# Block-diagonal products of a transformer block's training step regrouped from five 128-column blocks to six groups of whole heads

## The chip, the cores and the metric

The kernel runs on one core of one Trainium2 chip. The metric is the time of one launch on the device in microseconds (us), as the median of several executions; every execution quoted here ran at the full granted TensorE clock (1.00 in the records). Engines are named as in the profile: PE is TensorE's matmuls, PEld its weight loads, DVE VectorE, ACT ScalarE, POOL GpSimd, SP SyncE; a q behind a name is that engine's DMA queue.

## The reference, cut to what matters

One sequence of S = 2048 rows and D = 640 columns goes through a linear-attention block (32 heads of 20 columns) and a gated feed-forward block. The outputs are the result and the gradients of all inputs.

```python
def _A_ref(x, wqkv, wo):                       # H = 32, Dh = 20
    q, k, v = ...                              # x @ wqkv, cut into heads
    pq, pk = phi(q), phi(k)
    kv  = jnp.einsum("bhsd,bhse->bhde", pk, v) # one 20 x 20 block for each head
    z   = jnp.einsum("bhsd->bhd", pk)
    num = jnp.einsum("bhqd,bhde->bhqe", pq, kv)
    den = jnp.einsum("bhqd,bhd->bhq", pq, z)[..., None] + 1e-6
    return (num / den) ... @ wo
...
h  = x + _A_ref(_layernorm(x), A_wqkv, A_wo)
h2 = h + _B_ref(_layernorm(h), B_w_gate, B_w_up, B_w_down)
# outputs: h2 and its vjp for x, wqkv, wo, w_gate, w_up, w_down
```

The kernel never makes v. It uses that kv is a 640 x 640 matrix with 32 small blocks on its diagonal, KV, and folds it into weights: W2 = KV wo (forward), WK2 = dKV wv-transposed (backward), and the weight gradients dwo = KV-transposed G and dwv = Y dKV, where Y and G are sums over the sequence.

## The kernel before: the parts concerned

The 640 columns are cut into five blocks of 128. A head has 20 columns, so 128-column blocks cut heads: every block has to be multiplied with all blocks that share a head with it, and each of these matmuls streams full chunks of 320 columns, mostly against zeros.

```python
def head_range(i):                      # heads that block i touches
    h_lo = (i * P) // Dh
    h_hi = (i * P + P - 1) // Dh
    return Dh * h_lo, min(D, Dh * (h_hi + 1))
def overlapping(c0, c1):
    return [i for i in range(DT) if not (head_range(i)[1] <= c0 or head_range(i)[0] >= c1)]
...
for i in range(DT):                     # W2: 26 matmuls of 320 columns
    js = overlapping(i * P, (i + 1) * P)
    ps = mm("ps_w2")
    mm_row(ps, lambda k: KVT[:, js[k], i * P:(i + 1) * P], lambda k, n0, n1: wo[:, js[k], n0:n1], len(js))
    nc.scalar.copy(out=half(W2[:, i, :]), in_=row(ps))
dm(3)                                   # three tiles of dm = dh2 wd^T, ready work for PE
...
for t in range(ST + 2):                 # the loop behind it, on 16 tiles
    if t < ST:
        ...
        mm_row(ps, ..., lambda i, n0, n1: W2[:, i, n0:n1], DT)      # ps_a
        nc.vector.tensor_tensor(out=half(xr[:]), in0=row(ps), in1=half(xr[:]), op=ALU.add)
        nc.scalar.dma_start(out=scr_h1_v[:, t, :], in_=xr[:])       # store of the first residual
        ...
        dm(1)                           # ten matmuls and a ScalarE eviction
...
def dwo(j):                             # 26 matmuls of 320 in all; dwv is alike, with 30
    is_ = overlapping(j * P, (j + 1) * P)
    ps = mm("ps_dwo")
    mm_row(ps, lambda k: KV[:, is_[k], j * P:(j + 1) * P], lambda k, n0, n1: G[:, is_[k], n0:n1], len(is_))
    nc.scalar.copy(out=half(ev[:]), in_=row(ps))
```

`mm` takes the next of four PSUM accumulators in turn.

Of the kernel before, what the change touches and what calls it, by code (L numbers as in the profile page):

```python
# [20 lines left out]
def kernel(  # L21
# [69 lines left out]
    scr_KVT = dram.tile([D, D], BF16, name="scr_KVT")  # L91
# [4 lines left out]

    def head_range(i):
        h_lo = (i * P) // Dh
        h_hi = (i * P + P - 1) // Dh
        return Dh * h_lo, min(D, Dh * (h_hi + 1))  # L100

    def overlapping(c0, c1):
        return [i for i in range(DT) if not (head_range(i)[1] <= c0 or head_range(i)[0] >= c1)]
# [8 lines left out]
    def mm_row(ps, lhs, rhs, n, start=True, stop=True, by_k=False):  # L112

        steps = [(ci, k) for ci in range(2) for k in range(n)]
        if by_k:
            steps.sort(key=lambda x: x[1])
        for ci, k in steps:
            nc.tensor.matmul(ps[:, ci, :320], lhsT=lhs(k), rhs=rhs(k, *NCH[ci]),  # L118
                             start=(start and k == 0), stop=(stop and k == n - 1))

# [58 lines left out]
    wvo = strips.tile([P, 2, DT, D], BF16, name="wvo", tag="S")  # L179
# [8 lines left out]
    nc.scalar.dma_start(out=x_tm[0][:, 0, 320:640], in_=x_v[:, 0, 320:640])  # L188
    w_k = A_wqkv[:, D:2 * D].rearrange("(k p) n -> p k n", p=P)
    nc.sync.dma_start(out=wqk[:, 0:3, D:2 * D], in_=w_k[:, 0:3, :])  # L190
    load_x(nc.sync, 1, 2)
# [12 lines left out]
    def load_3():  # L204
        for t0 in range(4, ST, 2):
            yield load_x(nc.sync, t0, t0 + 2)
        yield nc.sync.dma_start(out=wvo[:, 0], in_=A_wqkv[:, 2 * D:3 * D].rearrange("(k p) n -> p k n", p=P))
        yield nc.sync.dma_start(out=wvo[:, 1], in_=A_wo.rearrange("(k p) n -> p k n", p=P))
        yield load_wdT(wdT, 0)
        for c in range(4):  # L210
            yield nc.sync.dma_start_transpose(out=dh2T[:, :, c * 512:(c + 1) * 512], in_=go_flat[c * 512:(c + 1) * 512, :])
        yield load_wdT(wdT, 1)
        yield load_wdT(wdT3, 3)
# [13 lines left out]
    mask = const.tile([P, DT, 160], BF16, name="mask")  # L227
# [12 lines left out]
    wv = wvo[:, 0]  # L240
    wo = wvo[:, 1]
# [13 lines left out]
    def ln1(t):  # L255
# [6 lines left out]
        if t == 0:  # L262
            ln1_stats(1)
            wait_for(nc.scalar.copy(out=xnT[:, t, 0:3], in_=tpv[:, 0:3]), load_3())
            nc.vector.tensor_copy(out=xnT[:, t, 3:5], in_=tpv[:, 3:5])
        else:
            nc.scalar.copy(out=xnT[:, t], in_=tpv)  # L267
# [107 lines left out]
    def masks():  # L375
# [9 lines left out]
        for i in range(DT):  # L385
            e0, e1 = head_range(i)
            pm = ps[:, i // 3, (i % 3) * 160:(i % 3) * 160 + e1 - e0]
            nc.tensor.matmul(pm, lhsT=E[:H, i * P:(i + 1) * P], rhs=E[:H, e0:e1], start=True, stop=True)
        for i in range(DT):
            e0, e1 = head_range(i)  # L390
            pm = ps[:, i // 3, (i % 3) * 160:(i % 3) * 160 + e1 - e0]
            nc.scalar.copy(out=mask[:, i, :e1 - e0], in_=pm)
# [10 lines left out]
    def normalise(t):  # L403
# [8 lines left out]
        nc.vector.tensor_tensor(out=hb4(pq), in0=hb4(pq), in1=bc4(rall[:, t:t + 4, :]), op=ALU.mult)  # L412
        for tt in range(t, t + 4):
            nc.sync.dma_start_transpose(out=pqsT[:, :, tt * P:(tt + 1) * P], in_=pqa[:, tt, :])
# [8 lines left out]
    with tc.manual_schedule(engines={EngineType.PE, EngineType.DVE}):  # L423
        yk = strips.tile([P, 2, DT, D], BF16, name="yk", tag="S")
        Yt = yk[:, 0]
        KVT = yk[:, 1]
# [12 lines left out]
        nc.gpsimd.dma_start(out=mat_v(scr_Yt), in_=Yt)  # L439
        dm(1)  # L440
        for t in range(0, 12, 4):
            normalise(t)
        for t in range(3):
            load_xr(t)
        for j in range(DT):
            d0, d1 = head_range(j)
            ps = mm("ps_kvt")
            for i in range(DT):
                nc.tensor.matmul(ps[:, 0, :d1 - d0], lhsT=wv[:, i, j * P:(j + 1) * P], rhs=Yt[:, i, d0:d1],
                                 start=(i == 0), stop=(i == DT - 1))  # L450
            nc.vector.tensor_tensor(out=KVT[:, j, d0:d1], in0=ps[:, 0, :d1 - d0], in1=mask[:, j, :d1 - d0], op=ALU.mult)
        nc.gpsimd.dma_start(out=mat_v(scr_KVT), in_=KVT)
        normalise(12)

        W2 = wv
        dm(1)
        for i in range(DT):
            js = overlapping(i * P, (i + 1) * P)
            ps = mm("ps_w2")
            mm_row(ps, lambda k: KVT[:, js[k], i * P:(i + 1) * P], lambda k, n0, n1: wo[:, js[k], n0:n1], len(js))  # L460
            nc.scalar.copy(out=half(W2[:, i, :]), in_=row(ps))
        dm(3)
# [4 lines left out]
        for t in range(ST + 2):  # L467
# [16 lines left out]
            if 2 <= u <= DT + 1:  # L484
                nc.sync.dma_start(out=mat_v(scr_W2T)[:, :, (u - 2) * P:(u - 1) * P], in_=w2t)
            if 1 <= u <= DT:
                w2t = stage()[:, :DT, :]
                nc.sync.dma_start_transpose(out=w2t, in_=W2[:, u - 1, :])
# [125 lines left out]
    M = ctx.enter_context(tc.tile_pool(name="M", bufs=3))  # L614
    wpools.append(ctx.enter_context(tc.tile_pool(name="workC", bufs=7)))

    def mat(name):
        return M.tile([P, DT, D], BF16, name=name, tag="M")

# [4 lines left out]
    def tr_sb(dst, src, i):  # L624
        nc.sync.dma_start_transpose(out=dst[:, :, i * P:(i + 1) * P], in_=src[:, i, :])

    with tc.manual_schedule(engines={EngineType.SP, EngineType.Pool}):
        W2T = mat("W2T")
        nc.sync.dma_start(out=W2T[:], in_=mat_v(scr_W2T))
        woT = mat("woT")  # L630
# [69 lines left out]
    with tc.manual_schedule(engines={EngineType.SP, EngineType.DVE}):  # L700

        wqkvT = big.tile([P, 15, D], BF16, name="wqkvT", tag="B")
# [11 lines left out]
        for k in (2, 0, 1):  # L714
            for i in range(DT):
                with tc.issue_after(last_dh1T):
                    tr_piece(wqkvT[:, 5 * k:5 * k + 5, :], A_wqkv[:, k * D:(k + 1) * D], i)
# [3 lines left out]
        GT = mat("GT")  # L721
# [8 lines left out]
        dKVT = mat("dKVT")  # L730
        nc.vector.memset(dKVT[:], 0.0)
        for j in range(DT):
            d0, d1 = head_range(j)
            ps = mm("ps_dkvt")
            for i in range(DT):
                nc.tensor.matmul(ps[:, 0, :d1 - d0], lhsT=woT[:, i, j * P:(j + 1) * P], rhs=GT[:, i, d0:d1],
                                 start=(i == 0), stop=(i == DT - 1))
            nc.vector.tensor_tensor(out=dKVT[:, j, d0:d1], in0=ps[:, 0, :d1 - d0], in1=mask[:, j, :d1 - d0], op=ALU.mult)

        dzE = [wk("dzE"), wk("dzL")]  # L740
        ps = mm("ps_dz")
        for ci, (n0, n1) in enumerate(NCH):
            for t in range(ST):
                q = t % 4 * H
                nc.tensor.matmul(ps[q:q + H, ci, :320], lhsT=nS1[:, t, :], rhs=pqs_tm[:, t, n0:n1],
                                 start=(t < 4), stop=(t >= ST - 4))
        nc.vector.tensor_tensor(out=half(dzE[0][:]), in0=row(ps), in1=half(E[:]), op=ALU.mult)
# [8 lines left out]
        for i in range(DT):  # L756
            js = overlapping(i * P, (i + 1) * P)
            ps = mm("ps_wv2")
            mm_row(ps, lambda k: dKVT[:, js[k], i * P:(i + 1) * P], lambda k, n0, n1: wqkvT[:, 10 + js[k], n0:n1], len(js))
            nc.scalar.copy(out=half(WV2[:, i, :]), in_=row(ps))  # L760
            nc.sync.dma_start_transpose(out=WK2[:, :, i * P:(i + 1) * P], in_=WV2[:, i, :])
# [21 lines left out]
        G = mat("G")  # L783
# [10 lines left out]
        for t in range(ST + LAG):  # L794
# [13 lines left out]
            if 4 <= t < 4 + DT:  # L808
                tr_sb(G, GT, t - 4)
            if t == 4 + DT:  # L810
                KV = mat("KV")
            if 4 + DT <= t < 4 + 2 * DT:
                tr_piece(KV, scr_KVT, t - 4 - DT, overlapping((t - 4 - DT) * P, (t - 3 - DT) * P))
# [27 lines left out]
        dy = strips.tile([P, 2, DT, D], BF16, name="dy", tag="S")  # L841
        dKV = dy[:, 0]
        Y = dy[:, 1]

        def dwo(j):
            is_ = overlapping(j * P, (j + 1) * P)
            ev = wk("dwo", pool=j % 2)
            ps = mm("ps_dwo")
            mm_row(ps, lambda k: KV[:, is_[k], j * P:(j + 1) * P], lambda k, n0, n1: G[:, is_[k], n0:n1], len(is_))
            nc.scalar.copy(out=half(ev[:]), in_=row(ps))  # L850
            nc.gpsimd.dma_start(out=out_3[j * P:(j + 1) * P, :], in_=ev[:])

        def dwv(i):
            ev = wk("dwv", pool=1)
            ps = mm("ps_dwv")
            for ci, (n0, n1) in enumerate(NCH):
                ks = overlapping(n0, n1)
                for kk, k in enumerate(ks):
                    nc.tensor.matmul(ps[:, ci, :320], lhsT=Y[:, k, i * P:(i + 1) * P], rhs=dKV[:, k, n0:n1],
                                     start=(kk == 0), stop=(kk == len(ks) - 1))  # L860
# [11 lines left out]
        for t in range(ST):  # L872
# [22 lines left out]
            if t < DT:  # L895
                dwo(t)
            if 0 <= t - 3 < DT:
                tr_sb(dKV, dKVT, t - 3)
            if 0 <= t - 6 < DT:
                tr_piece(Y, scr_Yt, t - 6)  # L900
# [32 lines left out]
```

## Time and profile before

| | before |
|---|---|
| median, lowest, highest of 4 runs | 831.15, 831.02, 832.94 us |
| span of the profiled execution | 830.5 us |
| PE busy | 823.2 us (99%), 5533 matmuls |
| share of PE in the chain that ended last | 87% |

A kernel whose PE is busy for 99% of the span changes its time in two ways only: PE's matmuls become fewer or shorter, or PE waits less or more. So I cut the span at the starts of PE's stages. This is the windows view of the kernel before for four of them: W2 up to the first ps_a; the loop with ps_a; WK2 with the products behind it; and the last stretch with dwo and dwv. Columns: stretch, its length, busy time (and instructions) of PE, PEld, DVE, ACT, POOL, granted clock, DMA share, GB/s.

```profile
92.69:101.90 9.21, 9.21 (x58) 5.48 (x57) 6.90 (x5) 5.89 (x8) 0.00 (x0) 1.00 1.17 190
101.90:151.76 49.86, 49.86 (x322) 31.31 (x320) 33.43 (x74) 13.75 (x16) 12.91 (x30) 1.00 0.96 213
...
620.82:641.72 20.90, 20.77 (x185) 14.07 (x183) 9.25 (x25) 6.04 (x9) 1.12 (x2) 1.00 0.74 137
...
759.08:830.50 71.42, 68.66 (x520) 49.87 (x517) 13.52 (x18) 7.61 (x11) 15.04 (x28) 1.00 0.92 179
```

PE is busy for all of the first two and for all but 0.13 us of the third. (In the last, the idle 2.76 us are the tail behind the last matmul.)

### The profile page before, as it was taken

How to read it: one execution, taken by the hardware profiler on the slowest of the kernel's cores; microseconds unless marked ns; L12 is line 12 of the kernel's file. 1: busy time of each engine (PE TensorE's matmuls, PEld its weight loads, DVE VectorE, ACT ScalarE, POOL GpSimd, SP SyncE). 2: the span in 40 equal slices, each digit the busy share in tenths (PEclk: the TensorE clock that was granted, in tenths of full speed). 3: DMA queues.
4: the chain of work that ended last, by engine and by line, in shares of the span. 5: the costliest groups of instructions: out<-in, count | busy, mean ns of one | idle time of the engine just before them, and what ended most of it. 6: DMA issues, size and time to landing. Idle time of an engine off the chain costs nothing.

```text
span 830.5 us, 14069 instructions
## 1 busy us (share of the span) xinstructions
PE 823.2 (99%) x5533; PEld 527.7 (64%) x5533; DVE 446.4 (54%) x874; ACT 291.8 (35%) x414; POOL 187.4 (23%) x343
## 2 busy tenths in 40 slices
PE   8999999999999999999999999999999999999998
PEld 6766656554555555555656777777776777777776
DVE  6988766791077018800750157878874366621121
ACT  5982422670084126400831123223322133331101
POOL 2330022322312312221125302111300122113320
PEclk9999999999999999999999999999999999999999
DMA  9994889998659997994597767875597689799993
GB/s 290 210 350 105 165 181 240 281 235 202 146 118 217 211 208 154 204 242 97 109 242 172 251 171 194 213 197 165 132 230 137 110 163 169 154 245 199 216 224 89
DMA packets 281057, 158.53 MB, mean 191 GB/s; under 512 B 238976, under 2 KB 267456, under 8 KB 280992
## 3 DMA queue, kind: packets, MB, share of 16 engines
q1 hardware_dynamic: 254288, 81.30, 53.2%
q0 software_dynamic: 17888, 65.27, 25.5%
q10 hardware_dynamic: 8816, 11.08, 4.4%
q8 instruction: 43, 0.70, 0.4%
q14 instruction: 22, 0.18, 0.1%
HBM read 47.43 MB, written 53.46 MB: 121 GB/s over the span
## 4 chain that ended last, share of the span: by engine, by line
PE 87%; DVE 8%; DMA 3%; ACT 1%; issue 1%; POOL 0%; SPq 0%; ACTq 0%; DVEq 0%
PE ps_dw L590 20%; PE ps_dhn L118 14%; PE ps_dxn L824 8%; PE ps_o L886 7%; PE ps_dwqk L118 5%; PE ps_kq L118 4%; PE pg L518 4%; PE ps_dm L350 4%; PE pu L523 4%; PE ps_y L118 3%; PE ps_gt L642 3%; PE ps_dp L118 3%; PE ps_dk L118 3%; PE pdm L350 2%; PE ps_a L118 2%; DMA xr<-in_A_x_dram 1%
## 5 line engine op out<-in xcount | busy, mean ns | idle before, releaser
L118 PE MATMUL ps_dhn<-wgT,cols 128*128 128x320 bf16 x864 | 119.5, 299 | 0.0
L590 PE MATMUL ps_dw<-dd,hn 128*128 128x448 bf16 (+1 forms) x640 | 118.8, 346 | 0.0
L118 PEld LDWEIGHTS <-cols 128*128 128x128 bf16 x864 | 84.5, 98 | 32.9
L590 PEld LDWEIGHTS <-hn 128*128 128x128 bf16 x640 | 62.6, 98 | 54.2
L592 DVE CAST dwev<-ps_dw 128x896 bf16<-128x896 f32 (+3 forms) x12 | 10.9, 908 | 126.7 <-PE ps_dw L590 112.0
L592 ACT CAST dwev<-ps_dw 128x896 bf16<-128x896 f32 (+1 forms) x20 | 17.6, 879 | 163.5 <-PE ps_dw L590 140.4
L555 POOL DMA_DIRECT2D scr_dT<-stg x64 | 34.6, 541 | 166.6 <-DMA stg<-dd 165.4
L137 DVE CUSTOM_DVE_ANT_0 lb_a<-lb_dy,hn 128x640 bf16<-128x640 bf16 x32 | 26.4, 826 | 72.5 <-ACT lb_dy L135 72.5
L523 PE MATMUL pu<-wgu,hnT 128*128 128x448 bf16 (+1 forms) x320 | 63.6, 346 | 0.0
L518 PE MATMUL pg<-wgu,hnT 128*128 128x448 bf16 (+1 forms) x320 | 63.6, 346 | 0.0
L886 PE MATMUL ps_o<-wd,mT 128*128 128x320 bf16 (+2 forms) x462 | 62.7, 295 | 0.0
L590 PE MATMUL ps_dw<-m_s,dh 128*128 128x448 bf16 (+1 forms) x320 | 60.7, 346 | 0.8 <-DVE m_s L550 0.8
L824 PEld LDWEIGHTS <-ring 128*128 128x128 bf16 x480 | 47.0, 98 | 18.2
L886 PEld LDWEIGHTS <-mT 128*128 128x128 bf16 x462 | 44.5, 98 | 16.6
L824 PE MATMUL ps_dxn<-wqkvT,ring 128*128 128x320 bf16 x320 | 51.3, 299 | 0.0
L590 PEld LDWEIGHTS <-dh 128*128 128x128 bf16 x320 | 31.3, 98 | 28.2 <-issue 1.3
L518 PEld LDWEIGHTS <-hnT 128*128 128x128 bf16 x320 | 31.3, 98 | 27.1
L523 PEld LDWEIGHTS <-hnT 128*128 128x128 bf16 x320 | 31.3, 98 | 27.1
L350 PEld LDWEIGHTS <-dh2T 128*128 128x128 bf16 x320 | 31.3, 98 | 25.1
L118 PE MATMUL ps_kq<-wqk,xnT 128*128 128x320 bf16 x320 | 46.3, 299 | 0.9 <-ACT xnT L267 0.8
L350 PE MATMUL ps_dm<-wdT,dh2T 128*128 128x448 bf16 (+1 forms) x240 | 46.9, 344 | 0.0
L892 DVE TENSOR_TENSOR h1r<-ps_o,h1r 128x640 bf16<-128x640 f32 x15 | 12.4, 825 | 56.6 <-PE ps_o L886 46.7
(159 smaller groups left out, 1290.7 us busy)
## 6 DMA issues: line engine op xcount, KB each, us to landing
scr_dT<-stg POOLq DMA_DIRECT2D x48, 224.0 KB, 3.3
cols<-scr_dT POOLq DMA_DIRECT2D x6, 1728.0 KB, 8.3
scr_m<-m_s POOLq DMA_DIRECT2D x12, 448.0 KB, 4.6
cols<-scr_dT ACTq DMA_DIRECT2D x2, 1728.0 KB, 9.8
out_dram<-dwev POOLq DMA_DIRECT2D x30, 112.0 KB, 3.8
scr_dT<-stg POOLq DMA_DIRECT2D x16, 192.0 KB, 2.7
scr_pk<-pk SPq DMA_DIRECT2D x4, 640.0 KB, 7.2
scr_pq<-pqa SPq DMA_DIRECT2D x4, 640.0 KB, 7.7
```

The source lines that it names most:

```text
L118: nc.tensor.matmul(ps[:, ci, :320], lhsT=lhs(k), rhs=rhs(k, *NCH[ci]), start=(start and k == 0), stop=(stop and k == n - 1))
L137: nc.vector.tensor_tensor_reduce(out=a[:], in0=dy[:], in1=xhat, scale=1.0, scalar=0.0, op0=ALU.mult, op1=ALU.add, accum_out=sums[:, 1:2])
L350: nc.tensor.matmul(ps[:, c, :w], lhsT=dh2T[:, kt, (t + c) * P:(t + c + 1) * P], rhs=wdT[:, kt, o:o + w], start=(kt == 0), stop=(kt == DT - 1))
L518: nc.tensor.matmul(pg[:, c, :w], lhsT=hnT[:, kt, (t + c) * P:(t + c + 1) * P], rhs=wg[:, kt, 0:w], start=(kt == 0), stop=(kt == DT - 1))
L523: nc.tensor.matmul(pu[:, c, :w], lhsT=hnT[:, kt, (t + c) * P:(t + c + 1) * P], rhs=wg[:, kt, w:2 * w], start=(kt == 0), stop=(kt == DT - 1))
L555: nc.gpsimd.dma_start(out=scr_dT[t + c, :, KO[g]:KO[g] + GK[g], :], in_=stg[:, :GK[g], :])
L590: nc.tensor.matmul(ps[:, c, :w], lhsT=lhs(t), rhs=rhs(t), start=(t == 0), stop=(t == ST - 1))
L592: copy(out=ev[:, :len(parts), :w], in_=ps[:, :len(parts), :w])
L642: nc.tensor.matmul(ps[:, ci, :320], lhsT=dh1[:, t, i * P:(i + 1) * P], rhs=pqs_tm[:, t, n0:n1], start=(t == 0), stop=(t == ST - 1))
L824: nc.tensor.matmul(ps[:, ci, :320], lhsT=lhs[:, i, :], rhs=rhs[:, i, n0:n1], start=(k == 0 and i == 0), stop=(k == 2 and i == DT - 1))
L886: nc.tensor.matmul(po, lhsT=mT[:, t % 4, j, :], rhs=wd[:, j, n0:n1], start=(j == 0), stop=(j == FT - 1))
L892: nc.vector.tensor_tensor(out=half(h1r[:]), in0=row(ps), in1=half(h1r[:]), op=ALU.add)
```

## The change

Its intent: cut at head borders instead. Five groups of six heads (120 columns) and one of two heads (40) overlap nowhere, so each group meets only its own block. W2 and WK2 are made transposed, so that the narrow block is what streams (120 columns instead of two or three chunks of 320), and are turned back by DMA transposes.

```diff
+    OH = [120 * j for j in range(5)] + [D - P]      # where each group's 128 rows start
+    HC = [(0, 120)] * 5 + [(88, P)]                 # its own columns among them
+    def mm_heads(ps, lhs, rhs):
+        for j in range(HG):                         # 6 groups; one that crosses column 320 is cut
+            c0 = OH[j] + HC[j][0]
+            c1 = OH[j] + HC[j][1]
+            for ci, (n0, n1) in enumerate(NCH):
+                a, b = max(n0, c0), min(n1, c1)
+                if a < b:
+                    nc.tensor.matmul(ps[:, ci, a - n0:b - n0], lhsT=lhs(j), rhs=rhs(j, a - OH[j], b - OH[j]),
+                                     start=True, stop=True)
 ...
+    load_x(nc.scalar, 1, 2)                         # start: x tile 1 on ScalarE's queue
 ...
-    load_x(nc.sync, 1, 2)
 ...
         for i in range(DT):
-            js = overlapping(i * P, (i + 1) * P)
-            ps = mm("ps_w2")
-            mm_row(ps, lambda k: KVT[:, js[k], i * P:(i + 1) * P], lambda k, n0, n1: wo[:, js[k], n0:n1], len(js))
-            nc.scalar.copy(out=half(W2[:, i, :]), in_=row(ps))
-        dm(3)
+            ps = mm("ps_w2t")
+            mm_heads(ps, lambda j: wo6[:, j, i * P:(i + 1) * P], lambda j, a, b: KVT[:, j, a:b])
+            nc.scalar.copy(out=half(W2T[:, i, :]), in_=row(ps))
+            nc.sync.dma_start_transpose(out=W2[:, :, i * P:(i + 1) * P], in_=W2T[:, i, :])
+        tr_pqs(8)
+        normalise(12)
+        tr_pqs(12)                                  # 8 transposes of pqs, now behind W2's
+        dm(4)
 ...
-            mm_row(ps, lambda k: KV[:, is_[k], j * P:(j + 1) * P], lambda k, n0, n1: G[:, is_[k], n0:n1], len(is_))
+            for ci, (n0, n1) in enumerate(NCH):
+                nc.tensor.matmul(ps[:h1 - h0, ci, :320], lhsT=KV[:, j, h0:h1], rhs=G[:, j, n0:n1], start=True, stop=True)
 ...
-                    nc.tensor.matmul(ps[:, ci, :320], lhsT=Y[:, k, i * P:(i + 1) * P], rhs=dKV[:, k, n0:n1],
-                                     start=(kk == 0), stop=(kk == len(ks) - 1))
+            mm_heads(ps, lambda j: Y[:, j, i * P:(i + 1) * P], lambda j, a, b: dKV[:, j, a:b])
```

Cut here: KVT, dKVT and WK2 in the same manner, the mask (two small matmuls instead of five), dz split around dKVT, the transposes of G, Y and KV spread over other loops, one copy at the start moved from VectorE to ScalarE, the order of SyncE's queue in the W2 part fixed by the program with the stores of Yt and KVT on it, and buffers.

## The prediction

> **What bounds the kernel now.** I read the page first: busy times, then the chain by engine.
>
> ```profile
> PE 823.2 (99%) x5533; PEld 527.7 (64%) x5533; DVE 446.4 (54%) x874; ACT 291.8 (35%) x414; POOL 187.4 (23%) x343
> ...
> PE 87%; DVE 8%; DMA 3%; ACT 1%; issue 1%; POOL 0%; SPq 0%; ACTq 0%; DVEq 0%
> ```
>
> TensorE is busy 99% of the span and the chain that ended last runs through it for 87%. A busy PE could still be waiting inside its own spacing, so next the waits view of PE and the windows view:
>
> ```profile
> PE ps_warm L302 <- POOL ident masks.py:199: 1.4, 1, 1.4
> PE ps_t L260 <- DVE xn L256: 1.1, 3, 0.6
> PE ps_kq L118 <- ACT xnT L267: 0.8, 1, 0.8
> PE ps_dw L590 <- DVE m_s L550: 0.8, 2, 0.5
> ...
> 0.00:18.30 18.30, 14.71 (x133) 10.89 (x134) 11.36 (x36) 10.45 (x17) 4.60 (x14) 1.00 0.92 299
> 18.30:57.20 38.90, 38.90 (x320) 27.77 (x320) 34.73 (x97) 38.24 (x64) 15.17 (x28) 1.00 1.09 269
> ```
>
> All named PE waits together are 4.1 us, and 3.6 us of idle PE (18.30 less 14.71) lie in the first 18.3 us. So the time is the count of matmuls times their spacing. The chain in time order gives that spacing:
>
> ```profile
> 18.72 2.72 PE ps_kq L118 x20
> ...
> 68.59 1.89 PE ps_dm L350 x10
> ...
> 92.85 3.53 PE ps_w L118 x26
> ...
> 624.04 3.64 PE ps_wv L118 x26
> ...
> 772.01 0.81 PE ps_dwo L118 x6
> ...
> 804.61 0.81 PE ps_dwv L859 x6
> ```
>
> 2.72/20 = 136 ns for 320 columns, 1.89/10 = 189 ns for 448: 53 ns more for 128 columns, 0.414 ns a column, plus some 3 ns. The last four lines are the products that the change rewrites; each matmul there is a full 320 columns at 136 ns, though most of those columns meet zeros.
>
> **What the Trainium skill says.** "TensorE: Matmul & The Clock Gate", section "Back-to-back issue gap", has N/2.4 + 2.5 ns for a warm matmul: 135.8 and 189.2, as the trace has. From it 120 columns cost 52.5 ns. The same page, "Wait — 56ns, not 53.3ns?", puts a floor of about 25 ns on the spacing; nothing in this trace is narrower than 128 columns on a whole array, so that isn't shown here. Its section "LDWEIGHTS" has P/1.2 = 107 ns for a load of 128 columns; the trace disagrees as far as throughput goes: ten warm-up matmuls of 128 columns, each with its own load, take 0.72 us in the timeline, (0.72 - 0.22)/9 = 56 ns each. "Perfetto Trace Analysis", "Summary: the profiler window per engine type", says that the window of such a DMA leaves out the data movement; the trace agrees (a W2 transpose occupies the queue for 1.22 us and lands after 2.7), so I use time to landing.
>
> **The change, part by part.** The instruction orders of the two kernels show the same PE sequence outside the products named here.
>
> *Wide products.* W2 and WK2: 26 matmuls of 320 columns become 35: 20 of 120, 10 of 40 and 5 of 80 (two groups are cut at column 320). 26 x 136 = 3.53 us; after, 20 x 53 plus 15 narrow ones at, my estimate between the 25 and the 56 above, 40 ns: 1.66 us. Work falls by 1.87 us each. dwv goes from 30 x 136 = 4.08 to the same 1.66 us: 2.42 less. dwo goes from 26 to 12 matmuls of 320: 14 x 136 = 1.90 less. KVT and dKVT (25 of 140 or 160 columns, about 62 ns) become 25 x 53 + 5 x 40 = 1.53 us against 1.56: nothing. The mask loses three small matmuls, 0.2 us.
>
> *What of it reaches the end.* dwo and dwv stand between ps_o tiles of 3.80 us that wait for nothing, one eviction (0.69 us) each: all 1.90 and 2.42 count. The mask and KVT: the masking of KVT is DVE work behind the third normalise, whose last step ends at 89.72, just when the first mask product starts (89.64). PE coming 0.2 us earlier waits there: 0.
>
> *W2.* Here ScalarE limits.
>
> ```profile
> 86.89 2.83 DVE L412 TENSOR_TENSOR pqa<-pqa,rall 128x2560 bf16<-128x2560 bf16 x1
> 89.64 0.95 DVE L451 TENSOR_TENSOR yk<-ps_kvt,mask 128x140 bf16<-128x140 f32 x3
> 92.89 0.91 ACT L364 CAST dm<-ps_dm 128x896 bf16<-128x896 f32 x1 [2.75 <-PE ps_dm L350]
> 93.69 3.47 ACT L461 CAST wvo<-ps_w 128x640 bf16<-128x640 f32 x5
> 98.50 3.87 SPq L488 DMA_TRANSPOSE stg<-wvo  x3
> ```
>
> Let PE begin W2 at E (92.7 before). ScalarE copies dm until E+1.0, then evicts one block each 0.69 us: E+1.7, 2.4, 3.1, 3.8, 4.4. PE could be done at E+1.66, but there are four accumulators: block 4 waits for eviction 0, the next dm for eviction 1. PE goes on at E+2.4 instead of E+3.53: 1.1 us gained, not 1.87. New is that W2 itself now comes by five DMA transposes behind the evictions: the first issued at E+1.7, one each 1.25 us, the fifth at E+6.7, landing 2.7 us later at E+9.4. Before ps_a stand four dm (one more than before): E+2.4 + 4 x 1.89 = E+10.0. So it fits with 0.6 us to spare: no wait.
>
> *m_s.* PE waits 0.5 us for the elementwise at 187. That pipeline starts behind a table load at 154.07 which stands behind the last dm's eviction at 152.74; with one dm moved forward that eviction is gone and ScalarE starts some 1.4 us earlier, PE 1.1: 0.3 gained.
>
> *dKVT, dz, WK2.* dz is split around dKVT, which hides the eviction of GT (PE idles 0.25 us there now) and costs one more switch to 32 columns (0.2 to 0.3): 0. After dz ends at T (623.98 before) VectorE needs 2.24 us for dzE and dzL and then 16 x 0.356 us for the normalised x: the last is ready at T+8.05. The order shows 60 of the 96 dwqk matmuls behind it: T+8.05 + 60 x 0.136 = T+16.2, where before it was 641.72, T+17.74. WK2 gives 1.5 of its 1.87 us.
>
> *Start.* x tile 1 goes to ScalarE's queue and one copy from DVE to ACT. Tiles 1 and 2 come earlier, but tile 3 lands at 11.6 behind 800 KB of weights whose issue doesn't move, and all behind it is in program order: 0.
>
> *Sum.* 1.90 + 2.42 + 1.1 + 0.3 + 1.5 = 7.2 us; 831.3 - 7.2 = 824.1.
>
> **The rivals.** (1) A new wait for W2 before ps_a. For it: the slack is only 0.6 us, and pqsT transposes took up to 8.4 us to land in the stretch from 89.75, beside two stores of 800 KB. Against it: the KVT store is now later and small, and Yt's, issued near 88, takes 4.8 us. It would make 825 to 827. (2) Narrow matmuls bound by their weight loads, not by columns. At 98 ns (the length of one LDWEIGHTS row) 50 of them cost 50 x 58 = 2.9 us more: 827. Against it: the 56 ns of the warm-up. (3) The queue of SP as bound in the dk loop, where column transposes of GT and Yt join three others: four times 1.25 us in 5.43 us. Before had four too in ten of the sixteen steps without a wait of PE; so I expect none, but a late one would cost 1 to 3 us. (4) The start gains after all: up to half of the 3.6 us, 822.5.
>
> **Range and chances.** The centre has dwo, dwv and WK2, which are nearly certain (5.8 us), and W2 with m_s (1.4), which a wait could eat. Rivals 1 to 3 push up by up to 3 us, 4 down by 1.8, narrow ones at 25 ns by 0.5: 821.8 to 827.2. 2% would be 814.6, more than twice all the work removed; 2% slower needs a wait of 24 us, and nothing found makes one. Faster 0.02, same 0.97, slower 0.01.
>
> **What would show each step.** dwo twice 136 ns a group and dwv seven matmuls in about 0.33 us right behind ps_o, without idle PE; the W2 blocks spaced by evictions at 0.69 us, PE reaching ps_a some 10 us after the first block with no wait named for wvo; dwqk still in step with VectorE's 0.356 us. Wrong would be: a PE wait for a DMA at ps_a, at dxn or at dwo; 40-column matmuls far above 56 ns; PE reaching the dense stretch (18.3) much earlier.

## The result, and the profile after

The changed kernel takes 824.58 us in the median of four runs (823.56 to 825.51), against 831.15 for the kernel before: 6.57 us less. Ratios are the mean time of one kernel's fast runs over that of the other's of the same rounds, so not quite the ratio of these medians; here 0.9916, with a 95% interval of 0.9896 to 0.9935, that is 7.0 us less, 5.4 to 8.6. By the 2% line it is the same; it is faster by 0.8%. The predicted 824.1 was within 0.5 us.

The page of the changed kernel, busy times:

```profile
PE 815.3 (99%) x5549; PEld 522.8 (63%) x5549; DVE 444.0 (54%) x875; ACT 291.3 (35%) x412; POOL 187.2 (23%) x343
```

There are 16 matmuls more, and 7.9 us less of PE's busy time, for they stream fewer columns in all. The same four stretches in the windows view, and the first 18.3 us:

```profile
91.45:101.36 9.91, 9.51 (x77) 5.60 (x75) 6.83 (x4) 6.60 (x9) 0.00 (x0) 1.00 0.44 84
101.36:150.54 49.18, 48.13 (x311) 30.32 (x310) 32.61 (x73) 13.53 (x16) 12.34 (x29) 1.00 1.01 229
...
619.52:638.68 19.16, 18.82 (x198) 12.69 (x198) 9.53 (x26) 5.75 (x9) 2.01 (x3) 1.00 0.96 162
...
756.04:823.30 67.26, 64.38 (x511) 47.20 (x508) 13.51 (x18) 8.30 (x12) 15.74 (x29) 1.00 0.67 165
```
```profile
0.00:18.30 18.30, 15.79 (x143) 12.35 (x144) 12.07 (x38) 11.37 (x19) 4.62 (x14) 1.00 0.92 301
```

The first of these rows holds four dm tiles where before it held three; one tile is 1.89 us, so without it 9.91 is 8.02, 1.19 less than the 9.21 of before. The second row, one tile shorter, should be 49.86 - 1.89 = 47.97 us but is 49.18, and PE is idle in it for 1.05 us: a wait that before didn't have. The third is 1.74 shorter, the last 4.16 (4.28 up to the last matmul). In the first 18.3 us PE did 1.08 us more than before. The waits view of PE (total, times, longest) names the new wait, and the one for m_s that the prediction had hoped to shorten:

```profile
PE ps_dm L363 <- ACT dm L377: 1.0, 1, 1.0
...
PE ps_dw L607 <- DVE m_s L567: 0.6, 2, 0.3
```

The chain in time order around the rewritten gradients (start, length, engine, tile, line, number of matmuls):

```profile
760.01 0.27 PE ps_dwo L874 x2
760.28 3.80 PE ps_o L907 x28
...
780.38 0.38 PE ps_dwo L874 x2
...
799.88 0.29 PE ps_dwv L130 x7
800.17 3.81 PE ps_o L907 x28
```

A group of dwo is now two matmuls in 0.27 us (0.38 in the last, which has only 40 rows) where it was up to six in 0.81; a group of dwv is seven narrow ones in 0.29 us, and ps_o goes on right behind both. The timeline of the W2 stage:

```profile
91.45 2.20 PE L130 MATMUL ps_w2t<-yk,wvo 128*128 128x120 bf16 x35
92.45 3.09 ACT L475 CAST wvo<-ps_w2t 128x640 bf16<-128x640 f32 x5
93.17 6.50 SPq L476 DMA_TRANSPOSE wvo<-wvo  x5
93.80 7.73 PE L363 MATMUL ps_dm<-wdT,dh2T 128*128 128x448 bf16 x40
101.36 1.52 PE L111 MATMUL ps_a<-wvo,pqsT 128*128 128x320 bf16 x10
```

PE leaves W2 2.35 us after it began (91.45 to 93.80; predicted 2.4), the five evictions follow each other on ScalarE (3.09 us), and ps_a begins 9.91 us after W2 did (predicted 10.0) without a wait for W2.

So the parts that change PE's work came nearly as predicted, and two differences that the predicted sum didn't have, a start that was 1.04 us shorter (rival 4 had named it) and a wait of 1.21 us in the loop (no rival had), nearly cancelled each other. A prediction that is right by such a cancelling isn't yet understood, so most experiments went to these two.

This table has the lengths of PE's stretches (from the first matmul of one stage to that of the next, computed from the trace) for all profiled executions; the first column is the time to the first ps_z, a mark some way behind the start. Five stretches are left out, in which the two kernels differ by 0.24 us (the mask) or less than 0.1. In the changed kernel one dm tile of 1.89 us stands in the second column instead of the third, except in dm3.

```
             to ps_z  W2..ps_a  ps_a..pg  pg..ps_dhn  dkvt  WK2..dk  ps_o..last
before        57.27    9.21      49.87     308.23     3.16   17.74    68.44
before_b      56.60    9.21      49.87     308.23     3.16   17.74    68.44
after         56.23    9.91      49.18     308.05     2.87   16.30    64.16
after_b       56.64    9.91      47.97     308.15     2.87   16.30    64.16
after_c       56.73    9.91      47.98     307.54     2.86   16.30    64.16
x_sync        56.90    9.91      48.68     307.60     2.86   16.31    64.16
copy_dve      55.97    9.91      47.98     308.27     2.87   16.30    64.16
start_old     57.19    9.91      47.97     308.03     2.87   16.30    64.16
xr_early      56.57    9.91      47.98     308.33     2.86   16.30    64.16
h1_pool       56.56    9.91      47.98     307.55     2.87   16.30    64.16
dm3           56.25    8.02      51.55     307.62     2.86   16.30    64.16
pool_split    57.00    9.61      47.97     307.55     2.86   16.30    64.16
last_twice    56.70    9.91      47.97     307.55     2.87   16.30    67.27
```

For before, 49.87 - 1.89 = 47.98 is what the third column compares with: an undisturbed loop takes the same time in both kernels. Columns two, five, six and seven are the same to 0.01 us in every execution of the same code. The others differ between executions of the very same kernel.

### The profile page after: what moved, and what is told of

Its sections match the earlier page's. It is cut to its first block, busy times and chain, and to the rows that moved or that the text cites. A ratio compares the mean times of both kernels' runs of the same rounds, so it can differ in the third digit from the quotient of the medians.

```text
span 823.3 us, 14095 instructions
## 1 busy us (share of the span) xinstructions
PE 815.3 (99%) x5549; PEld 522.8 (63%) x5549; DVE 444.0 (54%) x875; ACT 291.3 (35%) x412; POOL 187.2 (23%) x343
## 4 chain that ended last, share of the span: by engine, by line
PE 85%; DVE 8%; DMA 3%; ACT 1%; SPq 1%; issue 1%; POOL 0%; ACTq 0%; DVEq 0%
PE ps_dw L607 20%; PE ps_dhn L111 14%; PE ps_dxn L852 8%; PE ps_o L907 7%; PE ps_dwqk L111 5%; PE ps_kq L111 4%; PE pg L535 4%; PE pu L540 4%; PE ps_dm L363 3%; PE ps_y L111 3%; PE ps_dk L111 3%; PE ps_gt L658 3%; PE ps_dp L111 3%; PE pdm L363 2%; DMA xr<-in_A_x_dram 1%; DVE m_s L562 1%
## 5 line engine op out<-in xcount | busy, mean ns | idle before, releaser
L852 PEld LDWEIGHTS <-ring 128*128 128x128 bf16 x480 | 46.9, 98 | 18.3
L147 ACT ACTIVATE lb_dy<-ps_dhn,rstd 128x640 bf16<-128x640 f32 x16 | 12.7, 793 | 87.6 <-PE ps_dhn L111 87.6
```

What stands on the lines that cost most here:

```text
L147: nc.scalar.activation(out=half(dy[:]), in_=row(ps), func=ACT.Copy, scale=rstd_col, accum_out=sums[:, 0:1])
L852: nc.tensor.matmul(ps[:, ci, :320], lhsT=lhs[:, i, :], rhs=rhs[:, i, n0:n1], start=(k == 0 and i == 0), stop=(k == 2 and i == DT - 1))
```

## The experiments

Eleven runs were made: eight edited kernels, the changed kernel twice more and the kernel before once more. All gave correct results. Unless said otherwise each is one profiled execution.

### Where the new wait comes from: the residual's store

My theory after the first result: the store of the first residual stands in ScalarE's in-order queue. In the trace it has to wait for completion counts that earlier transfers also use, the last of them one of the eight pqsT transposes that now run just there; dm's evictions stand behind it, and PE, with four accumulators, runs out of them. These are rows of ScalarE's timeline in the changed kernel, in its first profile:

```profile
109.09 0.34 ACTq L491 DMA_DIRECT2D scr_h<-xr  x1
109.47 0.91 ACT L377 CAST dm<-ps_dm 128x896 bf16<-128x896 f32 x1 [7.01 <-PE ps_a L111]
```

The last column says that nothing had run on ScalarE for 7.01 us: then the store is issued and an eviction follows at once; PE had ended those matmuls 4.7 us earlier. The chain of that execution has pqsT's fourth transpose landing at just that moment: it was issued at 104.58 and took 4.42 us. The bracket's "<-PE ps_a" is the profile's inference for the eviction itself, not for the store ahead of it. The rival of the next two expectations (theory X, late loads of x that hold VectorE) is answered by the same trace: the addition whose result this store writes out had ended at 103.74 us (102.92 + 0.82), 5.35 us before the store was issued.

```profile
102.92 0.82 DVE L490 TENSOR_TENSOR xr<-ps_a,xr 128x640 bf16<-128x640 f32 x1 [4.54 <-PE ps_a L111]
```

**h1_pool** puts that store alone on GpSimd's queue.

```diff
-                nc.scalar.dma_start(out=scr_h1_v[:, t, :], in_=xr[:])
+                nc.gpsimd.dma_start(out=scr_h1_v[:, t, :], in_=xr[:])
```

> The changed kernel with the stores of the first residual issued from GpSimd's queue in place of ScalarE's. In the changed kernel TensorE waits 1.2 us at the third dm of the loop for a copy on ScalarE, and that copy stood behind such a store, which was let go at 109.1, when a transpose of the scaled queries landed whose completion semaphore it uses next. Theory L (the store on ScalarE's in-order queue waits for a semaphore that the queue of transposes holds, and blocks the evictions): the 1.2 us go, from the first ps_a to the first pg it takes 47.97 in place of 49.18, the run is about 823.3 by the profile's span less 1.2, 822.1. Theory X (the residual's x tiles 3 and 4 are loaded too late, behind the eight transposes, and VectorE holds the accumulators): no change, since that order is untouched.

Measured: 823.62 us, the stretch from ps_a 47.98, no PE wait for dm. ScalarE's timeline there:

```profile
101.90 0.91 ACT L377 CAST dm<-ps_dm 128x896 bf16<-128x896 f32 x1 [0.98 <-PE ps_dm L363]
105.15 0.91 ACT L377 CAST dm<-ps_dm 128x896 bf16<-128x896 f32 x1 [2.34 <-PE ps_dm L363]
```

The eviction now follows PE with no lag (0.04 us), and so do all of the next ones. It wasn't spared by luck: in this execution, too, the fourth transpose was late (issued at 104.42, landed at 109.16), but nothing on ScalarE waited for it.

**xr_early** leaves the store on ScalarE but issues two more loads of x ahead of the transposes, which changes the transfers that the store's completion counts are shared with.

```diff
-        for t in range(3):
+        for t in range(5):
             load_xr(t)
 ...
-            if t > 0:
+            if t > 2:
                 load_xr(t + 2)
```

> The changed kernel with the x tiles 3 and 4 of the residual loaded before the transposes of W2 and of the scaled queries, as the kernel before did, stores left on ScalarE's queue. Theory X: the 1.2 us wait of TensorE at the third dm goes, 47.97 us from first ps_a to first pg. Theory L: it stays, about 49.2, give or take 0.3 as which semaphore comes next to the store changes with the order of issues.

Measured: 824.70 us, the stretch 47.98, no wait. This is what theory X forecast, and theory L's "it stays" failed; but L had left open which count the store would share, and the trace shows the answer. The store is issued at 104.67 us, 0.1 behind the landing of the second transpose (104.57), with whose count it now shares, and the eviction behind it begins at 105.16, again as soon as PE had ended; the fourth transpose, again late (109.52), holds nobody. So it isn't ScalarE's queue as such that costs time but what the store in it waits for: both ways of taking that wait away remove the lag.

**after_b and after_c** are the changed kernel again, without an edit; after_c was timed in five rounds.

> The changed kernel, unchanged, profiled once more. Theory on the wait of 1.0 to 1.2 us at the fifth and later dm tiles (ScalarE's in-order queue holds dm's evictions behind the store of the first residual, which waits for a slow pqsT transpose): PE's wait varies from execution to execution between 0 and 1.3 us, but ScalarE's first dm eviction in the loop again ends its lag of 2 to 5 us behind PE's matmuls. Rival, a fixed wait by the order of the code: again 1.0 to 1.2 us, to 0.2. Start: the first mark at 55.9 to 56.6 us.

> The changed kernel, unchanged, timed in the same rounds as the kernel with both edits. Theory (two differences between executions of one kernel, the x tiles' landing at the start and the dm wait behind the first residual's store, each 0 to about 1.2 us): runs spread over 823.5 to 825.5 with a median of 824.4 to 824.8, 6.3 to 7.0 below before; the kernel with both edits spreads less, since one of the two is gone. Rival (the dm wait is in nearly every timed run): median 824.9 or more. The profiled look has PE's dm wait anywhere from 0 to 1.3 us.

Measured: after_b 824.48 us, stretch 47.97; after_c 824.12 us in the median of five (823.80 to 825.17), ratio to before 0.9920 (0.9906 to 0.9933), stretch 47.98. No PE wait for dm in either. From ScalarE's timeline of after_b:

```profile
107.27 0.35 ACTq L491 DMA_DIRECT2D scr_h<-xr  x1
107.66 0.91 ACT L377 CAST dm<-ps_dm 128x896 bf16<-128x896 f32 x1 [4.79 <-DVE xr L490]
```

The lag is there in both, but of 2.5 us instead of 4.7, and four accumulators cover it. The kernel before had the same kind of lag, 1.8 and 2.0 us in its two profiles. So the wait of the first profile is no fixed part of the change (a run without it alone proves nothing, which is why the two edits above are judged by the lag): of seven executions with the store where the change has it (after, after_b, after_c, x_sync, copy_dve, start_old, last_twice), PE lost 1.21 us in one, 0.71 in one and nothing in five. What is fixed is a lag of 2.5 us or more. In all seven the store is issued 0.1 us behind the landing of the fourth of the eight transposes in this stretch. The sixteen pqsT transposes take 2.7 us to land in the median, and in each of three profiles (after, after_b, copy_dve) the slowest took 4.2 to 4.4; in the two executions with a wait (after, x_sync) it was that fourth one that took over 4 us (4.42 and 4.17), in the five without it took 2.7. The rival, a fixed wait by the order of the code, fell. Why a transpose lands late, and why not always the same one, stays open.

### The start

**x_sync** undoes the move of x tile 1 alone; **copy_dve** undoes the other edit of the start alone; **start_old** undoes both; **before_b** is the kernel before, once more.

```diff
 # x_sync
-    load_x(nc.scalar, 1, 2)
     nc.sync.dma_start(out=wqk[:, 0:3, D:2 * D], in_=w_k[:, 0:3, :])
+    load_x(nc.sync, 1, 2)
 # copy_dve
-            nc.scalar.copy(out=xnT[:, t, 3:5], in_=tpv[:, 3:5])
+            nc.vector.tensor_copy(out=xnT[:, t, 3:5], in_=tpv[:, 3:5])
```

> The changed kernel with one part undone: x tile 1 goes back to SP's queue, between the two loads of the key weights. Measured by the time at which TensorE begins the z sums (57.27 us before, 56.23 in the changed kernel) and by the landing of x tile 3 (11.61 and 10.57). Theory A, the queue of tile 1 decides: both go back by 1.0 us, to about 57.3 and 11.6. Theory B, the copy moved from VectorE to ScalarE decides: both stay within 0.2 of 56.2 and 10.6. Theory C, neither, the landing differs by chance from execution to execution: it falls anywhere between.

> The changed kernel with the other part of the start undone: the second copy of x tile 0 transposed goes back to VectorE, tile 1 stays on ScalarE's queue. Theory A (the queue): z sums still begin at 56.2, tile 3 lands at 10.6. Theory B (the copy): 57.3 and 11.6. Theory C (chance): anywhere between.

> The changed kernel with both edits of the start undone (x tile 1 back on SyncE's queue between the two weight loads, the second copy of the first tile's transpose back on VectorE). Theory that the change's start gains 1.0 us: first mark at 57.1 to 57.4 us, as before. Rival, chance of landing: 56.0 to 56.9, like the variants that undo one or none. The rest of the kernel is the changed one, so time 824 to 826.

> The kernel before, unchanged, profiled once more, to learn what of the start differs from one execution to the next. Before's third and later x tiles had their stats at 11.61 us and PE reached the dense stretch's first mark at 57.27 us; the changed kernel and its four variants reached it at 55.97 to 56.90. Theory that the start's gain belongs to the change (x tile 1 on ScalarE's queue): again 57.1 to 57.4, above all of the variants. Rival, that the start's 1.04 us is chance of the loads' landing: a value anywhere in 56.0 to 57.3, inside the variants' range. Also: no PE wait of over 0.3 us for dm's eviction at the first loop steps, as before (its ScalarE lag there was 1.8 us).

Measured: 824.79, 824.22, 825.19 and 831.74 us; first marks 56.90, 55.97, 57.19 and 56.60. The statistics of x's fourth tile, which wait for its load, show where it is decided. From the timeline of VectorE, first the kernel before, then before_b, each without the rows around it:

```profile
11.61 0.89 DVE L124 BATCH_NORM_STATS2 st<-x_tm 128x6 f32<-128x320 bf16 x2 [0.60 <-DMA x_tm<-in_A_x_dram]
```
```profile
10.61 0.88 DVE L124 BATCH_NORM_STATS2 st<-x_tm 128x6 f32<-128x320 bf16 x2
```

The same code began this step 1.0 us apart in two executions, and 0.67 us of that was left at the first mark. In all thirteen profiles the first ps_z comes 42.05 to 42.09 us behind the start of the fifth tile's statistics: the mark is decided by then, and nothing behind it differs. So the 1.04 us of the first comparison can't be read as an effect of the change. With all profiles together, the nine executions with x tile 1 on ScalarE's queue have marks of 55.97 to 57.00, mean 56.52; the four with it on SyncE's queue 56.60 to 57.27, mean 56.99. A gain of half a microsecond is likely, but the ranges overlap and thirteen executions don't settle it. Taken one by one, start_old came out as its theory had it and before_b as its rival (chance), and x_sync lay between its theories. The copy by ScalarE instead of VectorE shows no gain: copy_dve, without it, has the lowest mark of all, though that is one execution.

### How much room the transposed W2 has

**dm3** takes back the one dm tile that the change put in front of ps_a.

```diff
-        dm(4)
+        dm(3)
```

> Three dm tiles ahead of the first W2 consumer instead of four; the fourth goes back into the loop behind it. Theory that the chain of eviction, transpose and landing (W2's fifth piece lands near 101.1 us, PE reaches its consumer at 101.36 with four dm tiles of 1.89 us) leaves 0.2 to 0.6 us of slack: without the fourth tile PE arrives at about 99.5 and must wait some 1.6 us for wvo at ps_a, named in the waits view; the stretch from the W2 products to ps_a shrinks by 0.2 to 0.5 us only, not by 1.89. The loop gets one dm more (1.89), so the time rises by up to 1.6 us unless a later wait falls. Rival (the W2 transposes land much earlier than needed): no wait for wvo, the stretch shrinks by 1.89 and the time stays within 0.5 us of the changed kernel.

Measured: 825.53 us. Two rows of its timeline:

```profile
99.50 0.84 PE L111 MATMUL ps_a<-wvo,pqsT 128*128 128x320 bf16 x5
...
101.15 0.84 PE L111 MATMUL ps_a<-wvo,pqsT 128*128 128x320 bf16 x5 [0.81 <-DMA wvo<-wvo]
```

The first five matmuls of ps_a need only the first columns of W2 and run at once; the second five wait until 101.15, 9.67 us after W2's first matmul (91.48). With the fourth dm tile that half isn't reached before 10.59 us (101.36 + 0.68 - 91.45), so the room is 0.92 us. The expectation had a wait of 1.6 us right at the start of ps_a, with the stretch from W2 to ps_a only 0.2 to 0.5 us shorter. The stretch shrank by the full 1.89 us, as the rival had it; the wait came half a tile later and at about half the size, and another 0.55 us came at dm from the store's lag of 4.2 us in this execution. Together the loop lost 51.55 - 47.97 - 1.89 = 1.69 us, counted from start to start. The theory, a transposed W2 that is only just hidden, holds; the rival, that it lands long before it is needed, doesn't.

### What the narrow products cost

**last_twice** issues each matmul of dwo and dwv twice into the same place.

```diff
-            for ci, (n0, n1) in enumerate(NCH):
-                nc.tensor.matmul(ps[:h1 - h0, ci, :320], ...)
+            for _ in range(2):
+                for ci, (n0, n1) in enumerate(NCH):
+                    nc.tensor.matmul(ps[:h1 - h0, ci, :320], ...)
 ...
-            mm_heads(ps, lambda j: Y[:, j, i * P:(i + 1) * P], lambda j, a, b: dKV[:, j, a:b])
+            for _ in range(2):
+                mm_heads(ps, lambda j: Y[:, j, i * P:(i + 1) * P], lambda j, a, b: dKV[:, j, a:b])
```

> The changed kernel with every matmul of dwo and dwv issued twice into the same place (same result). It measures the marginal cost of the narrow products by itself: 12 more matmuls of 320 columns in dwo and 35 more of 120, 80 and 40 columns in dwv. Theory (column-bound, nothing hidden): dwo adds 12 x 136 = 1.63 us, so its groups' period beside a 3.80 us ps_o tile grows from 4.075 to 4.35; dwv adds 5 x 0.30 = 1.5 us, its period 4.10 to 4.40; the last stretch from the first ps_o grows from 64.16 to 67.3, the time to about 827.7. Rival (narrow matmuls bound by their weight loads of some 96 ns): dwv adds 35 x 0.096 = 3.4 us, last stretch 69.2. Rival (PE in this stretch waits for something else and products are hidden): less than 1 us in all.

Measured: 827.10 us, the last stretch 67.27, 3.11 us longer. The chain in time order:

```profile
758.77 0.54 PE ps_dwo L875 x4
...
800.28 0.59 PE ps_dwv L130 x14
```

Fourteen narrow matmuls take 0.59 us, seven took 0.29: 42 ns each, and nothing is hidden. The theory's 3.1 us holds; both rivals (5.0 us by weight loads, less than 1 us if hidden) fall. In the trace of the changed kernel the starts of dwv's matmuls are 51 to 53 ns apart behind 120 columns, 35 behind 80 and 27 to 29 behind 40.

### What paces the W2 stage, and a combined version

**pool_split** has the store on GpSimd's queue, as in h1_pool, and in addition W2's second and fourth eviction on VectorE.

```diff
-            nc.scalar.copy(out=half(W2T[:, i, :]), in_=row(ps))
+            (nc.vector.tensor_copy if i % 2 else nc.scalar.copy)(out=half(W2T[:, i, :]), in_=row(ps))
```

> Two edits to the changed kernel: the store of the first residual goes to GpSimd's queue (no transpose can hold ScalarE's evictions), and W2's second and fourth evictions go to VectorE. Theory (the W2 products are paced by ScalarE's evictions at 0.69 us, which is why only 1.1 of 1.87 us was gained): PE leaves the W2 products 0.6 to 0.8 us earlier, the stretch from W2 to ps_a falls from 9.91 to 9.1 to 9.3; the fifth W2 piece lands 0.9 us before it is needed now, so no wait for wvo takes its place. The stretch from ps_a to pg stays at 47.97 (no dm wait). Time 0.7 us below the changed kernel's undisturbed executions and 1 to 1.5 below its mean: about 823.0 to 823.7. Rival (the transposes bound it): a wait for wvo of 0.5 us or more at ps_a, the stretch plus wait stays at 9.9, time 823.8 or more.

Measured: 824.27 us in the median of four (823.98 to 824.72), ratio to before 0.9918 (0.9904 to 0.9931); W2 to ps_a 9.61. So 0.30 us were gained there instead of 0.6 to 0.8, and no wait for W2 came in its place. The timeline tells why:

```profile
92.42 0.91 ACT L377 CAST dm<-ps_dm 128x896 bf16<-128x896 f32 x1 [2.79 <-PE ps_dm L363]
93.01 1.68 DVE L475 CAST wvo<-ps_w2t 128x640 bf16<-128x640 f32 x2 [2.22 <-PE ps_w2t L130]
93.22 1.93 ACT L475 CAST wvo<-ps_w2t 128x640 bf16<-128x640 f32 x3
```

The first W2 block is still evicted by ScalarE, behind a dm eviction (until 93.92 us), and the fifth block needs that accumulator back (it starts at 93.97). The split sped up only what came after. That evictions pace the stage is confirmed in kind (taking two of five away shortens it); the size I had expected was wrong, and so was the time, 823.0 to 823.7. Nor does the version beat the changed kernel: after_c, in the same rounds, has 824.12 (just below the 824.4 to 824.8 expected of it) against its 824.27. The edits remove 0.3 us and an occasional wait, and this execution's start (57.00) was the latest of all kernels with the change's load order. Its runs spread over 0.74 us, those of after_c over 1.37, as expected if one of the two sources of spread is gone, though four and five runs are few to say so.

## Why the prediction was right, point by point

- **dwo and dwv.** Predicted 1.90 + 2.42 = 4.32 us; the stretch from ps_o to the last matmul fell by 68.44 - 64.16 = 4.28. From start to start dwv went from 4.08 to 1.50 us, 2.58 less, and dwo from 3.53 to 1.74, 1.79 less. What dwo lacks is in its last group, whose output has only 40 rows: 0.38 us instead of 0.27, and the ps_o tile behind it takes 3.90 instead of 3.80, a cost of 0.2 us that the prediction didn't have.
- **Narrow matmuls.** The term that was mis-sized is the estimate of 40 ns for 40 and 80 columns: it is 27 to 29 and 35. With rows of 120 columns at 51 to 53 ns as estimated (52.5), a dwv group is 0.29 us and not 0.33. Rival 2, bound by weight loads, fell in last_twice. Its cost of 2.9 us was also set too low: by its own premise the 110 matmuls of 120 columns would have taken 98 ns instead of 53 too, 5 us more.
- **W2.** Predicted 1.1 us of its 1.87, by evictions; it was 1.19 (9.21 less 8.02). No wait for W2, as predicted; its room, predicted as 0.6, is 0.92, since the first half of ps_a doesn't need the last transposes. Rival 1 was close: dm3 shows the wait that one dm tile less would bring.
- **WK2.** Predicted 1.5 us; the stretch gave 17.74 - 16.30 = 1.44. The step behind it shows in the trace: VectorE's last normalised tile ended at 630.41 us, 8.03 behind WK2's first matmul (622.38; predicted 8.05).
- **m_s.** Predicted 0.3 us. The stretch varies: 308.23 in both profiles of before, 307.54 to 308.33 in eleven with the change, on average 0.39 less, and that this is near 0.3 is luck. The step "that eviction is gone and ScalarE starts some 1.4 us earlier" failed: in its place the residual's last store stands right ahead of the table load, and in the changed kernel's first profile the load starts 2.13 us behind the first pg, where before had 2.31. Over the nine executions with that store on ScalarE's queue it is 1.41 to 2.40; PE then waits 0.33 to 0.62 us for m_s where it is 2.13 or more, and not at all where it is 1.71 or less. With the store on GpSimd's queue (h1_pool, pool_split) the load starts within 0.1 us of pg and the wait is gone, so this is the same store's doing once more. ScalarE's timeline, the changed kernel and h1_pool (first pg at 150.54 and 149.68):

```profile
152.31 0.33 ACTq L491 DMA_DIRECT2D scr_h<-xr  x1
152.67 1.28 ACT L556 ACT_TABLE_LOAD   x1 [2.49 <-DVE xr L490]
```
```profile
149.75 1.28 ACT L556 ACT_TABLE_LOAD   x1 [0.43 <-ACT dmst L377]
```

- **Mask, KVT, dKVT, dz.** Predicted 0. The mask with KVT gave 0.2 and the stretch with dKVT 0.29 us, of which 0.09 came back in the stretch ahead of it. These terms were rounded to zero too early; none is large.
- **SyncE's queue in the dk loop.** The stretch of dk is 117.36 us in both kernels; rival 3 fell.
- **The start.** The step "all behind it is in program order: 0" failed as it stood: the time to the dense stretch isn't fixed by the program order but by when x's tiles land, which differs by 0.67 us between executions of one kernel. A gain of about half a microsecond (rival 4) is likely and not settled. (Rival 4's 822.5 should have been 822.3, 1.8 below the centre.)
- **The step that was missing.** Nothing in the prediction looked at who else stands behind the pqsT transposes once they move into the loop. Rival 1 named their long landing but applied it to W2 alone; the one who waited was a store on ScalarE's queue, and behind it dm's evictions. It costs nothing in five executions of seven and up to 1.2 us in the others. In the first profile the short start nearly hid this wait in the total; that a total with both in it comes within 0.5 us of the forecast is in part luck.

Summing the stretches that don't vary gives 0.24 - 0.05 + 1.19 - 0.09 + 0.29 + 1.44 + 4.28 = 7.30 us (the first two are the mask and the step behind KVT, not in the table), with m_s 7.7, less a mean of (1.21 + 0.71)/7 = 0.27 us for the wait: 7.4. The timed runs say 7.0 (5.4 to 8.6) and, in the rounds of after_c, 0.0080 x 830.95 = 6.6 (5.6 to 7.8). Both contain 7.4. (The likely half microsecond of the start isn't in this sum; 7.9 would lie in the first interval and just outside the second.) That the medians of the timed runs differ by only 6.6 to 6.8 may be since the two profiled executions of before, with spans of 829.8 and 830.5 us, were slow ones for that kernel, whose nine timed ones in the last call have a median span of 829.0; which of its stretches is shorter in those, no profile shows.

## What to carry to other kernels

When matmuls are many and few columns are useful, cut at the borders of the structure and let the narrow operand stream. In dwv, where nothing else set the pace, the gain was that of the columns removed (2.58 us); in W2 evictions and in WK2 VectorE let only 1.19 and 1.44 us of an estimated 1.87 through. When transfers are moved to a new place, ask for each in-order queue which of its entries waits for one of them and what stands behind that entry. And profile the same kernel twice before explaining a microsecond: two differences of 1.0 and 1.2 us in the first pair of traces were in good part chance, and hid each other in the time.

## What the Trainium skill lacked or had wrong

- "TensorE: Matmul & The Clock Gate", section "Back-to-back issue gap", gives about 81 ns for each matmul as the sustained figure of a stream of load and matmul pairs with 128 columns, and calls N/2.4 + 2.5 too low there. Here such pairs run 56 ns apart at 128 columns in the warm-up, 51 to 53 at 120 and 35 at 80, which is that formula (55.8, 52.5, 35.8).
- The same page's floor of about 25 ns (section "Wait — 56ns, not 53.3ns?") fits, also with a weight load of 128 columns for each matmul: 27 to 29 ns at 40 columns, where the formula alone would give 19.2. Its "LDWEIGHTS" section gives P/1.2, 107 ns for such a load, and doesn't say whether loads overlap each other. Here they do: each shows as 95 to 98 ns in the trace, and within a group of dwv they start 28 to 53 ns apart.
- No page that I found speaks of the spread of a DMA's time to landing between executions: the fourth tile's statistics began 1.0 us apart in two executions of the same kernel, and of sixteen pqsT transposes with a median of 2.7 us in the changed kernel the slowest took 4.2 to 5.6 in eleven profiles of it and its variants, not always the same one.
- No page that I found says in so many words that a store in a compute engine's queue, waiting for completion counts that transposes of another queue also use, holds the engine's evictions: lags of 1.8 to 4.7 us here, 0.04 with the store on GpSimd's queue.
